# Two dense layers after attention: late part in units of 512 tokens, first product by seven half products, new priorities

## Chip, cores and metric

The kernel runs on one core of a Trainium2 chip. The metric is the device time of one execution in microseconds. The kernel before takes 1067.36 us, the median of three runs (1065.95 to 1068.06).

## The reference

Attention over 4 batches, 8 heads, 576 tokens and 64 elements a head, with a mask by blocks of 64 tokens, and then two dense layers on the 2304 tokens of all batches, 512 wide outside and 2048 wide inside. The weights come as 64-bit floats.

```python
scores = np.where(block_i >= block_j, scale * q @ k.T, -1e9)     # per batch and head, blocks of 64
attn = softmax(scores); x = (attn @ v), heads side by side       # (2304, 512)
# layer 1
h = x @ w_in                                                     # (2304, 512) @ (512, 2048)
g = np.maximum(h, 0.0) + alpha * np.minimum(h, 0.0)
x = g @ w_out                                                    # (2304, 2048) @ (2048, 512)
# layer 2, with weights of its own and no alpha
h = x @ w_in
g = h * (1.0 / (1.0 + np.exp(-1.702 * h)))
out = g @ w_out
```

## The kernel before

**Precision.** A matrix product is done as three: each operand is split into a high part and a low part (`hi_part`, L119, a ScalarE copy into the matmul's format; `lo_part`, L122, the difference, on VectorE or GpSimd), and high x high, high x low and low x high are added up in PSUM. A weight tile is loaded as 64-bit words (`load_w`, L132), made into 32-bit floats by one ScalarE and three VectorE instructions (`narrow`, L142) and split (`split_w`, L160).

**Stages.** The 2048 inner columns are 16 tiles of 128, counted by f. Under attention, layer 1 is done for f = 0 to 7 on blocks of 288 tokens (`gemm1`, L199, into tile `h`; `gate`, L211; `gate_split`, L222; `g2_half`, L237, into tile `x`); this partial sum of x goes to DRAM (`xa`). The late part follows: layer 1 for f = 8 to 15 and then layer 2 for all 16 f, both in six units of 384 tokens. A unit loads its input (`load_x`, L178), splits it whole (`split_x`, L184), and for each f runs 12 matmuls of the first product (four row blocks of 128, three splittings, 384 columns each, L207), the gate, the split of the gated tile, and the second product (`g2`, L636, matmuls at L653: four output tiles of 384 columns in layer 1, three of 512 columns in layer 2). `block_out` (L655) adds `xa` and stores to `x2s` in layer 1, or stores to `out` in layer 2.

**Buffers.** The late part has its own pools, which open when attention's close (`swap_pools`, L618). First products go to four PSUM banks in turn (`bank`, L195), second products gather in four more. Weight tiles of f = 0 to 7 lie in a pool of the whole kernel, those of f = 8 to 15 in a late one, and layer 2's tiles take over layer 1's places one by one.

**Order of the work.** Each step is entered with a planned place n and a kind (`at`, L115). The program is first written in the order of n; buffers of a ring are handed out in that order. Then `arrange` (L782) orders the instructions of every engine anew: it plays the program through with estimated costs (`cost`, L758) and, whenever an engine is free, takes from its ready instructions the one whose place, n + 0.1 x ORDER + SHIFT of its kind, is lowest. All DMAs are issued by SyncE (SP), in the order that this gives. While attention starts, "warm" matmuls (L579) on a constant tile fill TensorE.

Of the kernel before, what the change touches and what calls it, by code (L numbers as in the profile page):

```python
# [42 lines left out]
    "setup": 0, "swap": 0, "score": 1, "pv": 2, "prep t": 2.5, "warm": 2.6, "gemm1": 3, "gemm1 2": 3, "half": 3, "gemm2": 3.2, "soft": 3.5,  # L43
# [5 lines left out]
    "gate": -5.6, "gate 2": 3.5, "gemm1": 58, "gemm1 2": 12.5, "gemm2": 12.5, "half": 55.1, "half out": -40.2,  # L49
    "high": 14.8, "load alpha": 30.8, "load k": 48.3, "load q": -16.4, "load v": -13.4, "load w": 42,  # L50
    "load w 2": -8.5, "load x": 21.6, "narrow": 49, "narrow 2": 21.5, "norm": -15, "out": -55.1,
    "prep out": 29.6, "prep t": 14.3, "prep v": 33.9, "pv": 8.2, "pv out": -26.5, "rest": 11.7, "score": 53.6,
    "setup": -59.4, "soft": 5.6, "split g": -25.7, "split g 2": 33.6, "split w": 22.7, "split w 2": 22.6,
    "split x": 28.2, "split x 2": -47.3, "warm": 59.1,
# [5 lines left out]
def kernel(  # L60
# [21 lines left out]
    QB = 28  # L82
# [5 lines left out]
    NG = 6  # L88
    TA = 288
    TB = 384  # L90
    NB = NT // TB
# [15 lines left out]
    x2s = dram.tile([DM, NT], F32, name="x2s")  # L107

# [33 lines left out]
    def narrow(u):  # L142

        src = words[u]
        wi = src.bitcast(I32).rearrange("p (n t) -> p n t", t=2)
        wf = src.bitcast(F32).rearrange("p (n t) -> p n t", t=2)
        sq = raw.tile([128, 512], F32, tag="sq", name="sq")
        act.activation(out=sq, in_=wf[:, :, 1], func=ACTF.Copy, scale=2.0 ** -112)  # L150
        hi = sq.bitcast(I32)
        a = raw.tile([128, 512], I32, tag="wa", bufs=1, name="wa")
# [16 lines left out]
    def plan_w(z, u, n, lo, lag=2):  # L169
        at("load w" + z, n, lambda: load_w(u))  # L170
        at("narrow" + z, n + lag, lambda: narrow(u))
        at("split w" + z, n + lag + 1, lambda: split_w(u, lo))
# [3 lines left out]
    pend = {}  # L176

    def load_x(key, src, t0, n, pl, z):  # L178

        xl = pl.tile([128, KD, S if pl is blk else TB], F32R, tag=f"xl{z}", name="xl")[:, :, 0:n]  # L180
        sp.dma_start(out=xl.bitcast(F32), in_=src[:, t0:t0 + n].rearrange("(c p) t -> p c t", p=128))
        xb[key] = (xl.bitcast(F32), None, xl, n)

    def split_x(key, pl, z, lo, c=slice(0, KD)):  # L184
        r, xh, xl, n = xb[key]
        if xh is None:
            xh = pl.tile([128, KD, TB], F32R, tag=f"xh{z}", name="xh")[:, :, 0:n]
# [22 lines left out]

    def gate(key, layer, f):  # L211
        ps, n = pend[key, f]
        g = tmp_p.tile([128, TB], F32, tag="g", name="g")[:, 0:n]
# [8 lines left out]
    def gate_split(key, f, lo):  # L222
        g, n = pend.pop((key, f))

        w, z = (TA, f % NA) if key[0] == 0 else (TB, f % NG)
# [23 lines left out]
    def g2_half_out(key, d, t0, n):  # L249
        o = tmp_p.tile([128, TB], F32, tag="g", name="xo")[:, 0:n]  # L250
# [15 lines left out]
    def plan_x(i, n_split):  # L266
        def f(c):
# [4 lines left out]
            split_x((0, i), blk, 0, pool, slice(c, c + 1))  # L272
# [306 lines left out]
    def warm(cols):  # L579

        if "warm" not in st:
            st["warm"] = bank("warm")
        for _ in range(cols):
            pe.matmul(st["warm"], mk_l, mk_l.unsqueeze(1).to_broadcast([128, 3, 128]), start=True, stop=True)
# [30 lines left out]
    pb = ExitStack()  # L615
    late = {}

# [9 lines left out]
    NR = NF - NA  # L627
    for z in range(2 * NR):
        plan_w(" 2", (0, NA + z % NR, z // NR), t_end - QS + QA * z // NR, dve if z % 2 else pool)

    units = [(1, j) for j in range(NB)] + [(2, j) for j in range(NB)]
    seq = [(u, f) for u in units for f in (range(NA, NF) if u[0] == 1 else range(NF))]
    n2 = t_end + WT
    accs = {}

    def g2(u, f):  # L636
        layer, j = u
        gh, gl = gt.pop((u, f))
        oh, ol = W[layer - 1, f, 1]
        f0 = NA if layer == 1 else 0  # L640
        nd = KD if layer == 1 else TB // 128
        if f == f0:
            accs[u] = [late["o"].tile([128, DM], F32, tag=f"o{d}", name="acc") for d in range(nd)]
        for d in range(nd):
            sl = slice(128 * d, 128 * d + 128)
            if layer == 1:
                ps = accs[u][d][:, 0:TB]
                ops = ((oh[:, sl], gh), (oh[:, sl], gl), (ol[:, sl], gh))
            else:
                ps = accs[u][d]  # L650
                ops = ((gh[:, sl], oh), (gh[:, sl], ol), (gl[:, sl], oh))
            for z, (a, b_) in enumerate(ops):
                pe.matmul(ps, a, b_, start=f == f0 and z == 0, stop=f == NF - 1 and z == 2)  # L653

    def block_out(u):  # L655
        layer, j = u
        for d, ps in enumerate(accs.pop(u)):
            o = late["x"].tile([128, DM], F32, tag="o", bufs=2, name="o")
            if layer == 1:
                t = o[:, 0:TB]  # L660
                at_ = (slice(128 * d, 128 * d + 128), slice(TB * j, TB * (j + 1)))
                sp.dma_start(out=t, in_=xa[at_])
                dve.tensor_tensor(out=t, in0=ps[:, 0:TB], in1=t, op=ALU.add)  # L663
                sp.dma_start(out=x2s[at_], in_=t)
            else:
                act.activation(out=o, in_=ps, func=ACTF.Copy)  # L666
                sp.dma_start(out=out[TB * j + 128 * d:TB * j + 128 * d + 128, :], in_=o)

    LG = 2
    start = {}  # L670
    for z, (u, f) in enumerate(seq):
        n = n2 + z
        start.setdefault(u, n)
        plan_g1(" 2", n, u, u[0] - 1, f, pool)
        at("gemm2", n + LG, lambda u=u, f=f: g2(u, f))
        if f == NF - 1:
            at("out", n + LG + 1, lambda u=u: block_out(u))
    for y, u in enumerate(units):
        n = start[u]
        z = (y + 1) % 2  # L680
        at("load x", n - 6, lambda u=u, z=z: load_x(u, xs if u[0] == 1 else x2s, TB * u[1], TB, late["x"] if z else blk, z))
        at("split x 2", n - 3, lambda u=u, z=z: split_x(u, late["x"] if z else blk, z, dve))
    n3 = start[(2, 0)]
    for z in range(2 * NA):
        plan_w(" 2", (1, z // 2, z % 2), n3 - QB + QC * z // NA, dve if z % 2 else pool, 1)
    for z in range(2 * NR):
        plan_w(" 2", (1, NA + z // 2, z % 2), n3 - NR + z // 2 + 2 * (z % 2), dve if z % 2 else pool, 1)
# [70 lines left out]
def cost(eng, kind, ins, outs):  # L758
# [3 lines left out]
    if eng == "PE":  # L762
# [3 lines left out]
        each = 13.3 if mv.dtype == F32R else 2.7  # L766
        return cols / 2.4 + each, load / 1.2 + 13.3 if BYTES[w.dtype] == 4 else load / 4.8, cols * rows / 128, mode(w)
# [186 lines left out]
```

## Time and profile before

| | |
|---|---|
| median of three runs | 1067.36 us |
| span of the profiled execution | 1064.0 us, mean granted TensorE clock 0.988 |
| time of the profiled execution beside its span | not given apart; the runs' median lies 3.4 us above the span |
| instructions | 17161 |
| busy: TensorE matmul / weight load | 1014.2 / 931.0 us |
| busy: VectorE / ScalarE / GpSimd | 576.4 / 561.5 / 363.6 us |
| DMA | 120.28 MB, 47% of 16 engines' time |

One execution was profiled, and all rows come from it. Times are from the first instruction on. L207 is line 207 of the kernel. PE is TensorE's matmuls, PEld its weight loads, DVE VectorE, ACT ScalarE, POOL GpSimd, SP SyncE. Matmuls are pipelined, so the duration of one overlaps the next; the distance of their starts is what one costs. A tile's name stands without its number.

### The profile page before, as it was taken

How to read it: one execution, taken by the hardware profiler on the slowest of the kernel's cores; microseconds unless marked ns; L12 is line 12 of the kernel's file. 1: busy time of each engine (PE TensorE's matmuls, PEld its weight loads, DVE VectorE, ACT ScalarE, POOL GpSimd, SP SyncE). 2: the span in 40 equal slices, each digit the busy share in tenths (PEclk: the TensorE clock that was granted, in tenths of full speed). 3: DMA queues.
4: the chain of work that ended last, by engine and by line, in shares of the span. 5: the costliest groups of instructions: out<-in, count | busy, mean ns of one | idle time of the engine just before them, and what ended most of it. 6: DMA issues, size and time to landing. Idle time of an engine off the chain costs nothing.

```text
span 1064.0 us, 17161 instructions
## 1 busy us (share of the span) xinstructions
PE 1014.2 (95%) x6454; PEld 931.0 (87%) x6454; DVE 576.4 (54%) x1029; ACT 561.5 (53%) x1324; POOL 363.6 (34%) x334
## 2 busy tenths in 40 slices
PE   7777889989999999999999999999999999999998
PEld 4555788979899999999999999999999999999997
DVE  7899898678877756778872247822111121111110
ACT  6787888778888865554542335423232232322222
POOL 3354523223323435544442244422222222222221
PEclk8999999989999999999999999999999999999999
DMA  8899899899978764445551234401010010100000
GB/s 186 187 223 203 188 208 188 176 158 167 181 158 161 153 141 127 152 152 178 182 194 60 89 107 147 148 1 60 1 50 11 1 60 1 51 10 1 30 1 30
DMA packets 257283, 120.28 MB, mean 113 GB/s; under 512 B 213936, under 2 KB 250800, under 8 KB 257200
## 3 DMA queue, kind: packets, MB, share of 16 engines
q1 hardware_dynamic: 257200, 119.18, 47.0%
q8 instruction: 51, 0.84, 0.3%
q14 instruction: 32, 0.26, 0.1%
HBM read 68.82 MB, written 18.87 MB: 82 GB/s over the span
## 4 chain that ended last, share of the span: by engine, by line
PE 64%; DMA 1%; DVE 1%; ACT 1%; issue 0%; ACTq 0%; DVEq 0%
PE h L207 31%; PE acc L653 28%; PE x L245 1%; PE x L246 1%; PE x L247 1%; PE pv L519 1%; DMA xa<-xo 1%; PE sc L441 0%; DMA out_dram<-o 0%; DVE hl L494 0%; DVE g L216 0%; ACT hl L484 0%; ACT o L666 0%; DVE wl L123 0%; DVE wa L153 0%
## 5 line engine op out<-in xcount | busy, mean ns | idle before, releaser
L123 POOL TENSOR_TENSOR gs<-g,gs 128x384 fp32r<-128x384 f32 (+1 forms) x208 | 222.8, 1072 | 483.8 <-ACT gs L120 475.5
L207 PE MATMUL h<-xh,wh 128*128 128x384 f32 (+1 forms) x832 | 271.2, 326 | 6.1 <-ACT xh L120 3.4
L207 PE MATMUL h<-xh,wl 128*128 128x384 f32 (+1 forms) x832 | 269.5, 324 | 0.0
L219 DVE TENSOR_TENSOR g<-g,h 128x384 f32<-128x384 f32 x96 | 53.1, 553 | 301.8 <-ACT g L218 301.8
L653 PE MATMUL acc<-wh,gs 128*128 128x512 f32 x576 | 194.6, 392 | 0.0
L207 PE MATMUL h<-xl,wh 128*128 128x384 f32 x576 | 193.1, 335 | 0.0
L207 PEld LDWEIGHTS h<-xh,wh 128*128 128x128 f32 x832 | 156.2, 188 | 14.5 <-ACT xh L120 4.5
L218 ACT ACTIVATE g<-h 128x384 f32<-128x384 f32 x96 | 47.2, 492 | 213.7 <-PE h L207 210.0
L207 PEld LDWEIGHTS h<-xh,wl 128*128 128x128 f32 x832 | 156.3, 188 | 0.1
L120 ACT ACTIVATE gs<-g 128x384 fp32r<-128x384 f32 (+1 forms) x208 | 103.4, 497 | 83.8 <-DVE g L219 50.0
L653 PEld LDWEIGHTS acc<-wh,gs 128*128 128x128 f32 x576 | 108.1, 188 | 20.3 <-DVE o L663 0.2
L653 PE MATMUL acc<-wl,gs 128*128 128x512 f32 x288 | 113.7, 395 | 0.0
L207 PEld LDWEIGHTS h<-xl,wh 128*128 128x128 f32 x576 | 108.1, 188 | 4.1
L216 DVE SCALAR_TENSOR_TENSOR g<-g,nalph,h 128x288 f32<-128x288 f32 (+1 forms) x112 | 61.7, 552 | 71.0 <-ACT g L215 69.1
L653 PE MATMUL acc<-gs,wh 128*128 128x384 f32 x384 | 97.5, 334 | 0.0
L519 PE MATMUL pv<-pt,vp 128*128 128x256 f16 (+2 forms) x960 | 84.5, 242 | 8.9 <-DMA pt<-hl 7.6
L215 ACT ACTIVATE g<-h 128x288 f32<-128x288 f32 (+1 forms) x112 | 49.0, 440 | 83.2 <-PE h L207 75.5
L494 DVE SCALAR_TENSOR_TENSOR hl<-e,stat,hl 64x64 f16<-64x64 f32 (+4 forms) x160 | 89.5, 591 | 5.1 <-ACT hl L484 3.8
L123 POOL TENSOR_TENSOR wl<-sq,wh 128x512 fp32r<-128x512 f32 x40 | 58.6, 1464 | 97.1 <-ACT wh L120 92.4
L464 ACT ACTIVATE e<-sc,stat 64x64 f32<-64x64 f32 (+4 forms) x160 | 82.4, 517 | 5.6 <-DVE stat L456 5.1
L484 ACT ACTIVATE hl<-e,stat 64x64 f16<-64x64 f32 (+4 forms) x160 | 78.2, 551 | 9.8 <-DVE stat L474 4.6
L519 PEld LDWEIGHTS <-vp 128*128 128x128 bf16 x960 | 62.5, 99 | 20.0 <-DMA pt<-hl 9.5
(65 smaller groups left out, 1735.2 us busy)
## 6 DMA issues: line engine op xcount, KB each, us to landing
rw<-in_moe_w_in_dram SPq DMA_DIRECT2D x32, 512.0 KB, 3.9
rw<-in_moe_w_out_dram SPq DMA_DIRECT2D x32, 512.0 KB, 3.6
nat_q<-in_q_dram SPq DMA_DIRECT2D x24, 288.0 KB, 4.1
nat_k<-in_k_dram SPq DMA_DIRECT2D x16, 288.0 KB, 3.3
nat_v<-in_v_dram SPq DMA_DIRECT2D x16, 288.0 KB, 3.8
xa<-xo SPq DMA_DIRECT2D x32, 144.0 KB, 2.1
o<-xa SPq DMA_DIRECT2D x24, 192.0 KB, 2.4
xl<-xs SPq DMA_DIRECT2D x6, 768.0 KB, 4.4
```

The source lines that it names most:

```text
L120: act.activation(out=dst, in_=src, func=ACTF.Copy, scale=scale_)
L123: eng.tensor_tensor(out=dst, in0=src, in1=hi.bitcast(F32), op=ALU.subtract)
L207: pe.matmul(ps, st_[:, sl], mv[:, c], start=z == 0, stop=z == 3 * KD - 1)
L215: act.activation(out=g, in_=ps, func=ACTF.Relu, scale=-1.0)
L216: dve.scalar_tensor_tensor(out=g, in0=g, scalar=nalph[:, f:f + 1], in1=ps, op0=ALU.mult, op1=ALU.add)
L218: act.activation(out=g, in_=ps, func=ACTF.Sigmoid, scale=1.702)
L219: dve.tensor_tensor(out=g, in0=g, in1=ps, op=ALU.mult)
L464: act.activation(out=eo, in_=v[:, h] if len(heads) > 1 else v, func=ACTF.Exp, scale=-1.0, bias=stat[0:m, 0, a:a + 1], accum_out=stat[0:m, ...
L484: act.activation(out=o, in_=e, func=ACTF.Copy, scale=r)
L494: dve.scalar_tensor_tensor(out=hl_part(j, 1, m, nk, h), in0=es[h][0:m, off:off + nk], scalar=stat[0:m, 2, 2 * a + h:2 * a + h + 1], in1=hl ...
L519: pe.matmul(o, l, r, start=z == 0, stop=z == len(ops) - 1)
L653: pe.matmul(ps, a, b_, start=f == f0 and z == 0, stop=f == NF - 1 and z == 2)
```

## The change

Three parts, which come together.

*Units and first product.* The late units have 512 tokens (four of them and a last one of 256), and the f are taken in pairs. For a pair the weights form 2 x 2 blocks: rows of the input width in two halves, columns the two f; the unit's input forms 2 x 2 blocks of its row halves and of its two halves of 256 tokens. Strassen's scheme gives the four blocks of the result from seven products of combinations in place of eight. Four products (`first_half`) go to the two banks of a pair, a copy and two sums are taken from there (`snap`, ScalarE and GpSimd), three more products are added into the same banks (`second_half`), and VectorE adds the copies (`sums`). Each product is 2 row blocks x 3 splittings of 256 columns. The unit of 256 tokens needs four products. The second product now has 512 columns in layer 1 as well, and is planned two jobs (a job is a pair on a unit) behind the first.

*Combinations.* The seven combinations of a pair's weights are formed and split once on chip (`comb`) and stored to DRAM, 256 KB each. Layer 1's four pairs are fetched once and stay; layer 2's eight pairs are fetched anew for every unit into three slots that reuse places of older weights. The weights of layer 1's pairs are planned during attention (n = 75, 89, 103, 117; before at about 133). The input's seven combinations are formed for each unit (`comb_x`); its raw tile has one buffer, which the attention part uses too.

*Order.* Nearly all SHIFT values are new, those of attention and of the early blocks too, and `cost` counts a matmul of this format as 0.4515 ns a column and its weight load as 109 ns.

```diff
-    "gate": -5.6, "gate 2": 3.5, "gemm1": 58, "gemm1 2": 12.5, "gemm2": 12.5, "half": 55.1, "half out": -40.2,
...
+    "comb 2": 305.0, "comb 3": -66.8, "first": -168.3, "gate": -94.1, "gate 2": -2.7, "gemm1": 32.1,
...
-    NG = 6
+    NG = 4
     TA = 288
-    TB = 384
-    NB = NT // TB
+    TB = 512
+    TH = TB // 2
...
+    def comb(l, j, i):
+        a, b = (words[l, f, 0] for f in fpair(l, j))
+        a11, a12, a21, a22 = a[:, 0:256], a[:, 256:512], b[:, 0:256], b[:, 256:512]
+        two_ = {0: (a11, a22, ALU.add), 1: (a21, a22, ALU.add), 4: (a11, a12, ALU.add), 5: (a21, a11, ALU.subtract),
+                6: (a12, a22, ALU.subtract)}
...
+        t = slot(j, i) if kept else raw.tile([128, 2, 256], F32R, tag="wc", bufs=2, name="wc")
+        lo = pool if i % 2 else dve
...
+            (dve if i % 2 else pool).tensor_tensor(out=r, in0=x, in1=y, op=op)
...
+        hi_part(t[:, 0], r)
+        lo_part(lo, t[:, 1], r, t[:, 0])
...
+            sp.dma_start(out=wcs[l][j][i], in_=t.bitcast(F32).rearrange("p h c -> p (h c)"))
...
+    def load_wc(p):
...
+        for i in range(7):
+            if n == TB or i in (2, 3, 5, 6):
+                t = slot(j if l == 0 else (p - P2) % NSL, i)
+                sp.dma_start(out=t.bitcast(F32).rearrange("p h c -> p (h c)"), in_=wcs[l][j][i])
...
+    UO = (0, 1, 4, 2, 3), (0, 1, 2, 3, 4)
...
+    def load_x(u):
+        l, t0, n, key = u
+        xr = blk.tile([128, KD, TB], F32, tag="xl0", name="xr")[:, :, 0:n]
...
+    def comb_x(u, i):
...
+                x = late["x"].tile([128, 2, TH], F32, tag="xt", bufs=2, name="xt")
+                y, y2, op = two_[i]
+                pool.tensor_tensor(out=x, in0=y, in1=y2, op=op)
...
+        pl, tag = (blk, ("xlb", "xh0")[i]) if i < 2 else (late["x"], f"xc{i}")
+        t = pl.tile([128, 2, 2, TH], F32R, tag=tag, name="xc")
+        hi_part(t[:, 0], x)
+        lo_part(dve, t[:, 1], x, t[:, 0])
...
+    def prod(ps, p, i, y, first, last):
...
+        for c in range(2):
+            sl = slice(128 * c, 128 * c + 128)
+            for st_, mv in ((w[:, 0, sl], x[:, 0, c]), (w[:, 0, sl], x[:, 1, c]), (w[:, 1, sl], x[:, 0, c])):
+                pe.matmul(ps, st_, mv, start=first and z == 0, stop=last and z == 5, skip_group_check=True)
...
+    def first_half(p):
+        g, e = bank("ga"), bank("ep")
...
+            prod(g[:, 0:TH], p, 0, 0, True, False)
+            prod(g[:, TH:TB], p, 2, 2, False, True)
+            prod(e[:, 0:TH], p, 1, 1, True, False)
+            prod(e[:, TH:TB], p, 5, 5, False, True)
...
+    def snap(p):
...
+            act.activation(out=u, in_=g, func=ACTF.Copy)
+            act.activation(out=v, in_=e[:, 0:TH], func=ACTF.Copy)
+            pool.tensor_tensor(out=v, in0=u[:, TH:TB], in1=v, op=ALU.subtract)
+            pool.tensor_tensor(out=u[:, 0:TH], in0=u[:, 0:TH], in1=v, op=ALU.add)
...
+    def second_half(p):
...
+            prod(g[:, 0:TH], p, 6, 6, False, False)
+            prod(g[:, TH:TB], p, 4, 4, False, True)
+            prod(e[:, 0:TH], p, 3, 3, False, True)
...
+    def sums(p):
...
+            dve.tensor_tensor(out=u[:, TH:TB], in0=el, in1=v, op=ALU.add)
+            dve.tensor_tensor(out=u[:, TH:TB], in0=u[:, TH:TB], in1=gr, op=ALU.subtract)
+            dve.tensor_tensor(out=er, in0=er, in1=u[:, 0:TH], op=ALU.add)
+            dve.tensor_tensor(out=gl, in0=gl, in1=u[:, TH:TB], op=ALU.add)
...
+    seq_w = [(QB + QD * j, 0, j, None) for j in range(NPAIR[0])]
+    seq_w += [(t_end + 0.5 + y, 0, None, NA + y) for y in range(NR)]
+    n3 = start[2, 0]
+    seq_w += [(t_end + NR + 1 + (n3 - t_end - NR - 4) * j / NPAIR[1], 1, j, None) for j in range(NPAIR[1])]
+    seq_w += [(n3 - QC + 2 * f if f < NA // 2 else n3 + f - NA // 2, 1, None, f) for f in range(NF)]
...
-        each = 13.3 if mv.dtype == F32R else 2.7
-        return cols / 2.4 + each, load / 1.2 + 13.3 if BYTES[w.dtype] == 4 else load / 4.8, cols * rows / 128, mode(w)
+        time = cols * 0.4515 if mv.dtype == F32R else cols / 2.4 + 2.7
+        return time, load / 1.2 + 2.5 if BYTES[w.dtype] == 4 else load / 4.8, cols * rows / 128, mode(w)
```

## Rows read from the trace of the kernel before

**Rows 1.** Stretches: length, busy us (instructions) of each engine, TensorE clock, DMA share, GB/s.
```profile
0.00:105.00 105.00, 77.12 (x512) 52.20 (x513) 90.82 (x169) 76.66 (x194) 42.76 (x45) 0.92 0.92 198
105.00:404.00 299.00, 283.89 (x2397) 264.73 (x2396) 232.06 (x502) 243.90 (x673) 101.05 (x101) 0.99 0.86 170
...
454.00:664.00 210.00, 209.50 (x1209) 208.78 (x1209) 131.92 (x181) 92.81 (x171) 83.43 (x65) 1.00 0.43 139
664.00:1064.00 400.00, 394.91 (x1978) 357.02 (x1976) 82.06 (x127) 117.78 (x224) 105.83 (x98) 1.00 0.09 30
```
**Rows 2.** Chain of waits, 878 to 888 us: start, length, what.
```profile
878.99 2.10 PE h L207 x12
881.10 2.08 PE acc L653 x9
883.18 2.10 PE h L207 x12
```
**Rows 3.** Groups by line, TensorE: shapes, count, busy us, mean ns, idle before.
```profile
L653 PE MATMUL acc<-wh,gs 128*128 128x512 f32 x576 | 194.6, 392 | 0.0
L207 PE MATMUL h<-xh,wl 128*128 128x384 f32 x576 | 193.6, 336 | 0.0
L653 PE MATMUL acc<-gs,wh 128*128 128x384 f32 x384 | 97.5, 334 | 0.0
...
L207 PEld LDWEIGHTS h<-xl,wh 128*128 128x128 f32 x576 | 108.1, 188 | 4.1
```
**Rows 4.** Timeline of TensorE, 308.5 to 311 us: start, length, engine, line, tiles, shape.
```profile
308.65 0.60 PE L345 MATMUL tp<-ident,nat_q 128*128 128x128 f32 x4
...
309.69 0.29 PE L247 MATMUL x<-gs,wl 128*128 128x288 f32 x1
...
310.89 0.29 PE L247 MATMUL x<-gs,wl 128*128 128x288 f32 x1
```
**Rows 5.** Line 345 alone: duration ns min/median/max, first and last start us.
```profile
L345 PE MATMUL tp<-ident,nat_q x152: 270/273/473, 10.4 to 364.4; 128*128 128x128 f32 x152
```
**Rows 6.** Groups by line, the other engines, whole span.
```profile
L123 POOL TENSOR_TENSOR gs<-g,gs 128x288 fp32r<-128x288 f32 x64 | 60.7, 953 | 114.8 <-ACT gs L120 111.1 <-PE h L207 3.4
L123 POOL TENSOR_TENSOR wl<-sq,wh 128x512 fp32r<-128x512 f32 x40 | 58.6, 1464 | 97.1 <-ACT wh L120 92.4 <-PE acc L653 2.9 <-DMA nat_v<-in_v_dram 1.7
...
L155 DVE SCALAR_TENSOR_TENSOR wa<-sq,wa 128x512 int32<-128x512 int32 x64 | 61.2, 957 | 1.2
...
L153 DVE TENSOR_SCALAR wa<-sq 128x512 int32<-128x512 int32 x64 | 43.4, 678 | 11.5 <-ACT sq L150 10.4
L532 DVE SCALAR_TENSOR_TENSOR x<-pv,x 64x256 f32<-64x256 f32 x32 | 13.7, 427 | 22.0 <-ACT x L531 21.3
...
L666 ACT ACTIVATE o<-acc 128x512 f32<-128x512 f32 x18 | 10.7, 596 | 11.7 <-DMA out_dram<-o 7.8 <-PE acc L653 3.1
```
**Rows 7.** Tile xlb alone: duration ns min/median/max, first and last start us.
```profile
L207 PE MATMUL h<-xlb,wh x256: 288/294/429, 43.8 to 446.2; 128*128 128x288 f32 x128
L123 POOL TENSOR_TENSOR xlb<-x,xh x32: 790/816/1662, 42.7 to 426.8; 128x288 fp32r<-128x288 f32 x32
```
**Rows 8.** Line 247 alone, the last of a block's second product.
```profile
L247 PE MATMUL x<-gs,wl x256: 288/295/402, 128.7 to 462.6; 128*128 128x288 f32 x128
```
**Rows 9.** Stretches, line 153 on VectorE alone, one instruction for each weight tile narrowed.
```profile
0.00:400.00 400.00, 11.63 (x18) 0.97 0.88 179
400.00:470.00 70.00, 8.81 (x14) 1.00 0.47 146
```
**Rows 10.** DMA issues: count, KB each, median us from issue to landing.
```profile
xl<-xs SPq DMA_DIRECT2D x6, 768.0 KB, 4.4
...
out_dram<-o SPq DMA_DIRECT2D x18, 256.0 KB, 2.0
```
**Rows 11.** Timeline of TensorE at the end, 1052 to 1064 us.
```profile
1052.42 0.33 PE L207 MATMUL h<-xh,wl 128*128 128x384 f32 x1
...
1058.53 0.39 PE L653 MATMUL acc<-wh,gs 128*128 128x512 f32 x1
```

More of the change, by code (lines that the diff above doesn't have):

```diff
@@ L42 @@
 ORDER = {
-    "setup": 0, "swap": 0, "score": 1, "pv": 2, "prep t": 2.5, "warm": 2.6, "gemm1": 3, "gemm1 2": 3, "half": 3, "gemm2": 3.2, "soft": 3.5,
+    "comb 2": 6.5, "comb 3": 6.5, "load w 3": 9, "narrow 3": 7, "split w 3": 5.9, "load wc": 8.8, "first": 3, "second": 3, "snap": 2.7, "sums": 3.9, "setup": 0, "swap": 0, "score": 1, "pv": 2, "prep t": 2.5, "warm": 2.6, "gemm1": 3, "gemm1 2": 3, "half": 3, "gemm2": 3.2, "soft": 3.5,
     "out": 3.8, "gate": 4, "gate 2": 4, "pv out": 4.5, "prep out": 4.7, "norm": 5, "high": 5.1, "half out": 5, "split w": 5.9,
@@ L626, with fpair @@
     at("swap", t_end, swap_pools)
[L627 to L633, printed above, removed]
-    accs = {}
[L636 to L643, printed above, removed]
+    def fpair(l, j):
+        f = 2 * j + (NA if l == 0 else 0)
+        return f, f + 1
@@ new lines, in load_wc @@
+    def load_wc(p):
+        l, (_, t0, n, _), j = jobs[p]
+        if l == 0 and j in wc0:
+            wc[p] = wc0[j]
+            return
+        ts = []
+        for i in range(7):
+            if n == TB or i in (2, 3, 5, 6):
+                t = slot(j if l == 0 else (p - P2) % NSL, i)
+                sp.dma_start(out=t.bitcast(F32).rearrange("p h c -> p (h c)"), in_=wcs[l][j][i])
+            else:
+                t = None
+            ts.append(t)
+        wc[p] = ts
+        if l == 0:
+            wc0[j] = ts
@@ L644, in g2 @@
+    accs = {}
+    def g2(u, f, first, last):
+        l, _, n, key = u
+        gh, gl = gt.pop((key, f))
+        oh, ol = W[l, f, 1]
+        nd = KD if l == 0 else n // 128
+        if first:
+            accs[key] = [late["o"].tile([128, DM], F32, tag=f"o{d}", name="acc") for d in range(nd)]
         for d in range(nd):
             sl = slice(128 * d, 128 * d + 128)
-            if layer == 1:
-                ps = accs[u][d][:, 0:TB]
+            if l == 0:
+                ps = accs[key][d][:, 0:n]
@@ L678 @@
[L678 to L687, printed above, removed]
+    place = []
@@ new lines @@
+    n = n2
+    for p, (l, u, j) in enumerate(jobs):
+        start.setdefault(u[3], n)
+        place.append(n)
+        n += 2 if u[2] == TB else 1
+    place += [n, n + 1, n + 2, n + 3]
+    for p, (l, u, j) in enumerate(jobs):
+        n, key = place[p], u[3]
+        at("load wc", place[max(p - 2, 0)] - 4 * (p < 2), lambda p=p: load_wc(p))
+        at("first", n, lambda p=p: first_half(p))
+        at("snap", n + 0.3, lambda p=p: snap(p))
+        at("second", n + 0.9, lambda p=p: second_half(p))
+        at("sums", n + 1.3, lambda p=p: sums(p))
+        for y, f in enumerate(fpair(l, j)):
+            z = 2 * (p % 2) + y
+            at("gate 2", n + 1.4, lambda key=key, l=l, f=f: gate(key, l, f))
+            at("split g 2", n + 1.4, lambda key=key, f=f, z=z: gate_split(key, f, pool, z))
+            at("gemm2", place[p + 2] + 0.1 + 0.1 * y, lambda u=u, f=f, a=j == 0 and y == 0, b=j == NPAIR[l] - 1 and y == 1: g2(u, f, a, b))
+        if j == NPAIR[l] - 1:
+            at("out", place[p + 2] + 0.4, lambda u=u: block_out(u))
```

167 lines of the change are left out of this document (128 added, 39 removed).

## The prediction

> **What bounds the kernel now.** I read the table of stretches first [rows 1]. From 454 us to the end TensorE is busy 209.5 of 210 us and 394.9 of 400 us at a granted clock of 1.00 (the 2.4 GHz level), while VectorE, ScalarE and GpSimd are busy for 21 to 63% of these stretches. From 105 to 404 us TensorE is at 95%, ScalarE at 82%, VectorE at 78% and the DMA engines at 86%: there everything is tight, and the clock is 0.99. Only the first 105 us hold much idle TensorE time (28 us). The chain of waits says the same of the late part: 12 first products, 9 second products, 12, 9, with nothing between [rows 2]. So the late part is as long as its matmuls. The groups by line [rows 3] give their number: first product (L207) 3 x 576 = 1728 of 384 columns, second product (L653) 384 and, of its low weights, half as many again, 576 of 384 columns in layer 1, and 576 + 288 = 864 of 512 columns in layer 2.
>
> **Spacing of matmuls.** "Mean ns of one" (336, 392) overlaps its neighbours and is no price. The distance of starts is: 12 of 384 columns lie between 878.99 and 881.10 us, which is 175.8 ns each (period 4.19 us less 2.08, by 12), and 9 of 512 columns in 2.08 us, 231.1 ns each [rows 2]. Nine intervals of 288 columns in a loaded stretch span 309.69 to 310.89 us: 133.3 ns each [rows 4]. Per column that is 0.458, 0.451 and 0.463 ns: time goes with columns, with no visible constant.
>
> **The change, part by part.**
>
> *First product.* A pair of 128-wide slices of the hidden layer on 512 tokens needs 7 half products x 2 row blocks x 3 splittings = 42 matmuls of 256 columns, where the direct form has 24 of 512. The last unit of a layer has 256 tokens and takes 4 products, 24 matmuls. Layer 1 has 4 pairs, layer 2 has 8: 12 x (4 x 42 + 24) = 2304 matmuls of 256 columns (589,824 columns against 663,552). No matmul of 256 columns in this format is in the trace. From below its spacing is bounded by four transposes of 128 columns, which end 0.60 us after their first start and last 0.273 us each: (0.60 - 0.273)/3 = 109 ns [rows 4, 5]. From above by 133.3 ns, the spacing at 288. I take 117.2, which is 256 x 0.458, the price of the row at 384, the nearest that nothing disturbs (by the row at 288 it would be 118.5). Before: 1728 x 175.8 = 303.8 us. After: 2304 x 117.2 = 270.0 us (251 to 307). Gain 33.8 us (53 to a loss of 3). This is on the path, as nothing else fills the late part.
>
> The Trainium skill, page "TensorE: Matmul & The Clock Gate", section "Back-to-back issue gap", puts the warm gap at N/2.4 + 2.5 ns; this case's rows of 384 and 512 columns lie 8 and 7% above that. By the page the sum would be 1728 x 162.5 = 280.8 before and 2304 x 109.2 = 251.6 after, a gain of 29 us.
>
> *Second product.* Layer 1: 384 of 512 and 96 of 256 columns, 88.7 + 11.3 = 100.0 us, where 576 x 175.8 = 101.3 us stood. Layer 2 keeps 864 of 512. A gain of 1.3 us (0 to 2), which I count as nothing.
>
> *Evictions.* A full job (a pair on a unit) now has two copies on ScalarE and two GpSimd operations between its halves, and four VectorE operations before its gates. What hides this is the second product of the job two back, 24 x 231 ns = 5.5 us, which TensorE does meanwhile; a copy from PSUM of 512 columns takes 0.60 us [rows 6], so the wait between the halves is about 1.3 us with its signals. Four banks hold two jobs; a job takes 42 x 117.2 + 24 x 231.1 ns = 10.5 us. Its banks must be free again after one whole job of the other pair of banks; the chain after its second half (4 x 0.43 for the sums by the 256-column row, gates of about 0.6 on ScalarE and 0.85 on VectorE, twice a row of 256) is some 4 us. Covered, 0 us. Without the cover it would be 1.3 us in each of 48 full jobs, 62 us.
>
> *Loads on the other engines in layer 1.* Its late part will last 16 x 10.5 + 4 x 5.6 = 190 us. GpSimd: 32 low parts of 512 columns at 1.46 us, 32 differences of 256 at 0.85 (scaled from 288 at 0.953), 20 input sums at 1.46, 48 operations of layer 2's combinations at 0.85, some 6 weight splits and the small unit's low parts: 160 us, or 84% [rows 6]. VectorE: 54 us of sums and gates (3.4 a full job), some 26 weight tiles to narrow at 0.68 + 2 x 0.96 = 2.6 us [rows 6], the input's low parts 20, the combinations 19, the outputs 13: near 182 us if all of it fell in this stretch, though pairs 2 to 7 may come during layer 2, where a job needs only 3.4 of 10.5 us. It fits, with little room. I charge the nine changes of unit for this: the new input needs four of its seven combinations (about 4.5 us by these rows) within the 7.6 us of second product and second half that stand between its first use and the old one. In layer 1 the three that start on a busy GpSimd I put at 1.5 us each: 5 us in all (0 to 20).
>
> *Into the late part.* The input buffer of a unit is now the one that the last attention batch leaves, and two combinations lie where the last early block has its split input. Those splits are made up to 427 us, and its last first product starts at 446 [rows 7]; after it 16 us of second halves are left, to 462.6 us [rows 8]. Load (4.4 us, [rows 10]) and combinations fit beneath. 0 us (0 to 6).
>
> *Under attention.* The 8 weight tiles of layer 1's pairs and their 28 combinations have to be ready when the late part starts. So far 18 of the 64 tiles are narrowed before 400 us and 14 from 400 to 470 [rows 9]; the eight now have to come earlier: 8 x 2.6 us on VectorE, 28 combinations with some 9, 11 and 20 us on VectorE, ScalarE and GpSimd, and 14.7 MB to DRAM and back. From 105 to 404 us VectorE has 67 us free, ScalarE 55, GpSimd 198 [rows 1]. New priorities order all of it again. From below a gain: the TensorE time lost in the first 404 us is 43 us. From above a loss: 30 us if all VectorE work of it were added to attention. As it fits the gaps by rows I take 2 us of loss.
>
> *Reload in layer 2.* Each job fetches its seven combinations of 256 KB: 256 fetches, 67.1 MB, with inputs, outputs and weights 84.9 MB in 1536 x 117.2 + 864 x 231.1 ns = 379.7 us, or 224 GB/s. From 454 to 664 us the queue moved 139 GB/s at a share of 0.43, so 323 GB/s at full share; from 105 to 404 us, with short packets, 170 at 0.86, so 198 [rows 1]. The new packets are of 2 KB, like the outputs that land in 2.0 us [rows 10] and the stretch from 454 on, so I take 323: 263 of 380 us, hidden, with three slots of buffer. 0 us (0 to 49).
>
> The Trainium skill, page "DMA: Bandwidth & Descriptors", section "Bandwidth", asks for 1 MiB in a transfer and gives 138 GB/s at 64 KB and 341 at 1 MB; 256 KB would be about 240 by an estimate between them. That would still be hidden, 354 of 380 us, but with far less room than the rows give.
>
> *The end.* The last first product starts at 1052.42 us and the last second one at 1058.53 [rows 11]; a small last unit leaves 12 instead of 9 second products behind it and one eviction less. 0 us.
>
> Sum on the profiled execution: 1064.0 - 33.8 + 5 + 2 = 1037.2 us. The median of the runs, 1067.36, is 3.4 us above that span (the page shows no other time of this execution), so **1041 us**.
>
> **Rivals.**
>
> 1. *Weight load sets the pace at 256 columns.* A load of 128 columns lasts 188 ns in the rows [rows 3], longer than the new spacing, and two of them must overlap. For it: no 256-column row. Against: at 288 columns loads of 188 ns already go at 133 ns, at 128 columns matmuls at 109. At 125 ns, halfway to the upper bound, 2304 x 7.8 = 18 us are lost: 1059.
>
> 2. *Reload bounds layer 2 (slower).* If the fetches run at the 198 GB/s of the loaded stretch, layer 2 takes 84.9 MB/198 = 429 instead of 380 us: 1041 + 49 = 1090. It decides below 224 GB/s. Against: short packets made that rate, and these are long.
>
> 3. *Layer 1's combinations come late (slower).* Two buffers carry them; a step (0.85 + 0.4 + 0.85 us, then 2.0 us to land) takes about 2.3 us, a pair with its two narrowings 21. If they begin only at 404 us, as 14 of 16 tiles did before, the pairs end at 488 us, and the eight tiles of the second product behind them in the same buffers at 510, where gemm2 wants the first at 464: up to 45 us, 1086. It costs the whole gain from a delay of 26 us on. Against: the gaps of VectorE and ScalarE named above.
>
> 4. *The new order shortens the early part.* Of the 43 us lost there a quarter, 11 to 12 us, comes back: 1029. For it: 28 us lie in the first 105, where warm-up matmuls run beside. Against: VectorE and DMA at 86 and 92% there.
>
> **How the numbers follow.** Forecast 0.63 (1030 to 1053), rival 1 0.08, rival 2 0.05, rival 3 0.12, rival 4 0.12. The range reaches from rival 4's side to just under the time before: 1026 to 1066; beyond it lie rival 2, most of rival 3 and a little of rival 4. A measurement of this kernel tells about 0.2% (2 us) from no change. Faster: 0.63 + 0.12 + 0.07 + a quarter of rival 3 = 0.85; the same 0.03; slower 0.12.
>
> **What would show it.** Late first products 117 ns apart, 42 and 24 to a job of 10.5 us; TensorE near 100% from about 460 us; layer 2's DMA share near 0.7 with no TensorE wait for a fetch; late part some 33 us shorter and its start within 10 us of 454. Wrong: a spacing above 122 ns, waits for combination tiles, or TensorE gaps at the unit changes of more than 2 us each.

## Result and profile after

The changed kernel takes 1079.13 us, the median of four runs (1077.71 to 1083.54), against 1066.98 us for the kernel before on the same chip: a ratio of 1.0114, interval 1.0089 to 1.0139. It was forecast at 1041 and is slower by 12 us. The profiled execution has a span of 1077.3 us.

The table of stretches of the changed kernel, to be laid beside [rows 1] (same columns):

```profile
0.00:105.00 105.00, 75.76 (x478) 51.77 (x479) 86.29 (x163) 73.32 (x187) 41.28 (x45) 0.87 0.86 194
105.00:404.00 299.00, 274.97 (x2277) 252.52 (x2275) 253.21 (x539) 251.30 (x695) 115.35 (x119) 0.97 0.94 198
475.00:600.00 125.00, 119.02 (x804) 109.45 (x803) 99.97 (x150) 63.80 (x139) 87.69 (x86) 1.00 0.57 187
600.00:700.00 100.00, 95.60 (x614) 86.05 (x614) 73.97 (x121) 50.27 (x99) 69.05 (x66) 1.00 0.79 268
700.00:800.00 100.00, 94.45 (x580) 82.78 (x579) 75.69 (x113) 49.74 (x91) 58.86 (x48) 1.00 0.77 261
800.00:1070.00 270.00, 269.29 (x1656) 241.50 (x1656) 84.33 (x162) 99.70 (x193) 111.77 (x108) 1.00 0.52 164
```

Three things are to be seen. From 105 to 404 us TensorE started 2277 matmuls where it had started 2397: attention and the early blocks run late. From 475 to 800 us it is short of full in every row, where nothing was missing before. From 800 us on it is full, and the DMA engines are at 0.52.

The early part ends with the second product of the last early block, which [rows 8] put at 462.6 us. The same line alone, in the changed kernel:

```profile
L253 PE MATMUL x<-gs,wl x256: 288/296/382, 139.0 to 483.2; 128*128 128x288 f32 x128
```

So the early part ends 20.6 us later. (This line, one row in each kernel, is the measure of the early part in all that follows. Some late products already run ahead of it: about 6 us of them in the kernel before and in the changed one.) The last first product over the old input buffer moved alike, from 446.2 [rows 7] to 467.5:

```profile
L208 PE MATMUL h<-xlb,wh x256: 290/296/442, 45.6 to 467.5; 128*128 128x288 f32 x128
```

The late part, from the first late product to the last second product, went from 604.4 us (454.2 to 1058.5) to 598.9 (474.5 to 1073.4), not to some 575. Its groups by line are as counted beforehand, 1368 + 936 = 2304 half products and 864 second products of layer 2 (576 in the third line, 288 more with the low weights):

```profile
L740 PE MATMUL ga<-xc,ws 128*128 128x256 f32 x1368 | 188.6, 284 | 8.7 <-ACT u L764 4.1 <-DVE g L222 2.2 <-DVE g L225 1.9
L740 PE MATMUL ep<-xc,ws 128*128 128x256 f32 x936 | 132.2, 284 | 4.0 <-ACT xc L126 1.6 <-DVE g L225 1.3 <-ACT v L765 0.8
L815 PE MATMUL acc<-wh,gs 128*128 128x512 f32 x576 | 182.8, 392 | 2.2 <-DVE o L825 1.9 <-ACT o L828 0.3
```

Their distances are read from the chain of waits in the dense stretch (start, length, what), as in [rows 2]:

```profile
884.97 1.44 PE ga L740 x12
886.41 0.72 PE ep L740 x6
887.13 4.11 PE acc L815 x18
891.24 1.43 PE ga L740 x12
```

Twelve of 256 columns take 1.44 us, 120 ns each; 18 of 512 columns take 4.11 us, 228.3 ns each. From these the late part without a gap would be 2304 x 0.120 + 1248 x 0.2283 + 96 x 0.120 = 276.5 + 284.9 + 11.5 = 572.9 us. So 26 us of the 598.9 are stalls (some 2 us of these are early products that still run between the first late ones). The rows of 475 to 800 us show 15.9 us as idle (325 less 119.02, 95.60 and 94.45); most of the rest hides in "busy", since one matmul is shown with 284 ns for a distance of 120.

How one such stall comes about, from the chain of waits around 685 us:

```profile
682.11 0.32 SPq L688
682.52 0.48 SPq L688
683.09 4.56 DMA wc<-wc
687.78 0.75 POOL wc L647
688.58 0.30 issue
688.88 0.96 ACT sq L156 x2
689.99 0.59 ACT g L224
690.58 0.28 ACT v L765
690.91 0.98 PE ep L740 x6
```

SyncE issues fetches of reloaded combinations (L688, the last two are shown), and only then the store of a freshly formed one (wc<-wc, L655). That store takes 4.56 us to land; until then its buffer isn't free, GpSimd can't write the next combination (L647), ScalarE, whose order is fixed, stands behind GpSimd, and behind that stand a gate (g) and the copy out of PSUM (v) that TensorE's second half needs. TensorE waits 0.81 us here. Over 475 to 800 us ScalarE and VectorE wait along this way, and ScalarE for raw weight tiles (rw) too (engine, line, waited for: us in total, times, longest):

```profile
ACT wc L126 <- POOL wc L647: 23.4, 12, 7.7
ACT sq L156 <- DMA rw<-in_moe_w_out_dram: 21.8, 12, 4.5
...
DVE wc L129 <- ACT wc L126: 19.3, 15, 2.7
```

The first and the last line belong to the forming; its last store starts at 690.1 us, so nothing is formed from 700 us on. The middle line is another matter: 19.5 of its 21.8 us lie between 700 and 800 us. There ScalarE waits for raw tiles of layer 2's second product, which SyncE loads among the fetches.

The DMA issues of 600 to 700 us (count, KB each, us to landing) show fetches and stores beside each other, and the output rows that were to be their price, 2.0 us in [rows 10], far off:

```profile
ws<-wc SPq DMA_DIRECT2D x47, 256.0 KB, 4.2
wc<-wc SPq DMA_DIRECT2D x21, 256.0 KB, 3.4
```

From 475 to 600 us, with seven fetches only, the stores landed in 2.2 us (median), and TensorE had stalls all the same.

Early, the wait that is new lies between 200 and 250 us. That stretch of before and of after (columns as in [rows 1]):

```profile
200.00:250.00 50.00, 44.59 (x368) 40.36 (x367) 38.78 (x87) 40.19 (x116) 15.30 (x17) 0.93 0.88 158
```
```profile
200.00:250.00 50.00, 38.65 (x302) 33.51 (x302) 41.56 (x90) 39.62 (x116) 14.86 (x16) 0.86 0.97 208
```

66 matmuls fewer, and the granted clock falls with the idle time, from a mean of 0.93 to 0.86 (between the levels of 1.2 and 2.4 GHz). TensorE's own waits there say for what: the scores of the next attention step stand behind ScalarE's exponentials of an earlier one, first before, then after:

```profile
PE sc L441 <- ACT e L464: 0.4, 1, 0.4
```
```profile
PE sc L447 <- ACT e L470: 9.2, 4, 4.4
```

### The profile page after: what moved, and what is told of

Same layout as the page of the kernel before. It is cut to its first block, busy times and chain, and to the rows that moved or that the text cites. A ratio compares the mean times of both kernels' runs of the same rounds, so it can differ in the third digit from the quotient of the medians.

```text
span 1077.3 us, 19739 instructions
## 1 busy us (share of the span) xinstructions
PE 1001.1 (93%) x6934; PEld 892.5 (83%) x6934; DVE 722.1 (67%) x1313; ACT 627.2 (58%) x1492; POOL 522.9 (49%) x506
## 4 chain that ended last, share of the span: by engine, by line
PE 49%; DMA 11%; ACT 7%; DVE 7%; issue 3%; POOL 2%; SPq 0%; ACTq 0%; POOLq 0%; DVEq 0%
PE acc L815 20%; PE ga L740 12%; PE ep L740 8%; DMA wc<-wc 4%; DMA rw<-in_moe_w_out_dram 3%; DMA pt<-hl 2%; PE pv L525 2%; PE sc L447 2%; ACT hl L490 2%; PE h L208 2%; ACT e L470 1%; POOL gs L129 1%; PE x L251 1%; PE x L252 1%; DVE g L222 1%
## 5 line engine op out<-in xcount | busy, mean ns | idle before, releaser
L129 POOL TENSOR_TENSOR gs<-g,gs 128x512 fp32r<-128x512 f32 (+2 forms) x184 | 208.0, 1135 | 207.2 <-ACT gs L126 171.4
L740 PE MATMUL ga<-xc,ws 128*128 128x256 f32 x1368 | 188.6, 284 | 8.7 <-ACT u L764 4.1
L740 PEld LDWEIGHTS ga<-xc,ws 128*128 128x128 f32 x1368 | 177.5, 191 | 18.4 <-ACT u L764 4.8
L126 ACT ACTIVATE gs<-g 128x512 fp32r<-128x512 f32 (+2 forms) x184 | 98.1, 536 | 83.7 <-PE acc L815 65.8
L740 PE MATMUL ep<-xc,ws 128*128 128x256 f32 x936 | 132.2, 284 | 4.0 <-ACT xc L126 1.6
L740 PEld LDWEIGHTS ep<-xc,ws 128*128 128x128 f32 x936 | 122.8, 191 | 10.4 <-DVE g L225 2.8
L815 PE MATMUL acc<-gs,wh 128*128 128x512 f32 (+1 forms) x320 | 94.5, 371 | 1.8 <-DVE o L825 1.8
L208 PE MATMUL h<-xh,wh 128*128 128x288 f32 x256 | 78.0, 305 | 5.2 <-ACT xh L126 2.6
L251 PE MATMUL x<-gs,wh 128*128 128x288 f32 x256 | 76.7, 302 | 0.9 <-ACT gs L126 0.4
L252 PE MATMUL x<-gs,wh 128*128 128x288 f32 x256 | 77.1, 302 | 0.3 <-POOL gs L129 0.3
L208 PE MATMUL h<-xh,wl 128*128 128x288 f32 x256 | 77.0, 301 | 0.0
```

The costliest lines, as they stand in the source:

```text
L126: act.activation(out=dst, in_=src, func=ACTF.Copy, scale=scale_)
L129: eng.tensor_tensor(out=dst, in0=src, in1=hi.bitcast(F32), op=ALU.subtract)
L208: pe.matmul(ps, st_[:, sl], mv[:, c], start=z == 0, stop=z == 3 * KD - 1)
L251: pe.matmul(ps, oh[:, sl], gh, start=f == 0, stop=False)
L252: pe.matmul(ps, oh[:, sl], gl, start=False, stop=False)
L740: pe.matmul(ps, st_, mv, start=first and z == 0, stop=last and z == 5, skip_group_check=True)
```

## Experiments

All kernels are built by the same planner, which writes out each engine's order. In the first four and the last three it plans anew after the edit. In the five called "order as in the changed kernel" or "order kept" the order is planned for the whole program first and then kept, instruction by instruction, while some of it is left out.

Where the stages ended, from the line of the early second product alone in each kernel and from the first and last late product (us):

| kernel | ratio of times | early part ends | late part |
|---|---|---|---|
| before | 1 | 462.6 | 604.4 |
| after | 1.0114 | 483.2 | 598.9 |
| after, old priorities | 1.0314 | 494.9 | 612.6 |
| before, new priorities | 1.0222 | 489.5 | 604.3 |
| layer 1 direct | 1.0326 | 488.4 (20 us of late products ahead) | 627.4 |
| four buffers | 1.0378 | 485.4 | 620.9 |
| three pairs not prepared in layer 1 | 1.0098 | 477.3 | 602.2 |
| layer 2's combinations not formed | 1.0003 | 482.4 | 587.0 |
| no reload | 1.0040 | 487.3 | 589.6 |
| no copies and sums | 1.0125 | 482.6 | 600.4 |
| neither forming nor reload | 0.9915 | 482.9 | 579.5 |
| before, nudged | 1.0167 | 481.7 | 608.4 |
| after, nudged (two draws) | 1.0251, 1.0210 | 482.5, 483.3 | 611.5, 606.4 |

**The old priorities in the changed kernel.**

```diff
 SHIFT = {   # 25 kinds of the early part
-    "gate": -94.1, "gemm1": 32.1, "half": 28.7, ...
+    "gate": -5.6, "gemm1": 58, "half": 55.1, ...
```

> The changed kernel with the old priorities for the 25 kinds of step that attention and the early blocks are made of. Theory A (the longer early part comes from the work brought under attention: eight weight tiles, 28 combinations and their transfers): the last early second product stays near 483 us (before 462, after 483), time 1079 +- 4 us. Rival B (it comes from the new order of the early steps): it goes back to about 463 us, time about 1059 us.

Measured: 1100.16 us (1097.06 to 1103.99), ratio 1.0314, interval 1.0274 to 1.0353; the early part ends at 494.9. Neither theory: the old priorities don't bring the old order back, as the planner places the added work among the same steps. Why this order is later still was not followed.

**The new priorities in the kernel before**, the same lines the other way round, with no work added.

> The kernel before with the new priorities for the same 25 kinds, nothing else. Theory A: the last early second product stays within 4 us of 462, time 1067 +- 4 us. Rival B: it moves to about 480 us, time about 1085 us.

Measured: 1089.63 us, ratio 1.0222, interval 1.0191 to 1.0253. The late part is as before (604.3 us); the early part alone is 26.9 us longer. An order planned from other priorities costs more here than the whole early loss of the change.

```profile
L247 PE MATMUL x<-gs,wl x256: 290/295/380, 146.6 to 489.5; 128*128 128x288 f32 x128
```

**Layer 1's late part direct**, in units of 512 tokens; the half products in layer 2 alone.

```diff
+        if l == 0:
+            for f, ps in zip(fpair(l, j), (g[:, 0:n], e[:, 0:n])):
+                h, lo = W[l, f, 0]
+                for c in range(KD):
...
-    seq_w = [(QB + QD * j, 0, j, None) for j in range(NPAIR[0])]
+    for y in range(NR):
+        plan_w(" 2", (0, NA + y, 0), t_end - QS + 0.8 * y, dve if y % 2 else pool)
```

> The changed kernel with layer 1's late part in the direct form (512-token units, 12 matmuls of 512 columns a tile, weights loaded and split where the kernel before does it); layer 2 keeps its half products. Theory A: with nothing added under attention the early part ends near 463 us. Rival B: near 480 us. Theory C (late stalls of 26 us come from forming layer 2's combinations through two buffers, which blocks the in-order engines): TensorE still loses 10 us or more during layer 1. Rival D (they come from the copies and sums of each job): less than 5 us there. Time by A and C about 1060 us, by A and D about 1049, by B 1069 or more.

Measured: 1100.77 us, ratio 1.0326, interval 1.0303 to 1.0349. With no combination formed or stored under attention the early part ends at 488.4, later than in the changed kernel. But here its last steps stand behind 88 late products, where the changed kernel has 54 of half the length. Two of four lines, from 460 us to the end of the early part (columns as in [rows 3]):

```profile
L766 PE MATMUL ga<-xd,wd 128*128 128x512 f32 x48 | 11.4, 390 | 0.0
L836 PE MATMUL acc<-gs,wh 128*128 128x512 f32 x20 | 6.2, 389 | 0.0
```

At 228.3 ns these 88 are 20 us. By this estimate the early part alone takes 468 us, against 477 in the changed kernel (54 x 120 ns = 6.5 us taken off) and 456 in the one before (36 x 175.8 ns = 6.3 us taken off): without the added work it is 8 us shorter than in the changed kernel and still 12 us longer than before. The order is another one, so this doesn't settle how the 20.6 us divide. Theories C and D stay open as well: TensorE is busy for 120.63 of 125 us from 475 to 600 us and 96.20 of 100 to 700, and loses most, 18.2 us, between 700 and 800.

**Two more buffers for layer 2's combinations.**

```diff
-        t = slot(j, i) if kept else raw.tile([128, 2, 256], F32R, tag="wc", bufs=2, name="wc")
+        t = slot(j, i) if kept else raw.tile([128, 2, 256], F32R, tag="wc", bufs=2, name="wc") if l == 0 else \
+            (raw.tile([128, 2, 256], F32R, tag="wc", bufs=2, name="wc") if i % 2 else
+             late["x"].tile([128, 2, 256], F32R, tag="wd", bufs=2, name="wc"))
```

> The changed kernel with four buffers in place of two for the combinations of layer 2's weights (two of them from the late pool). Theory C: the stalls of TensorE between 475 and 800 us fall from about 26 us to about 10, time about 1063 us. Rival D: they stay, time 1079 +- 4 us.

Measured: 1107.34 us, ratio 1.0378, interval 1.0339 to 1.0418, the slowest of all. The plan moved everywhere (the early part ends at 485.4, the late one is 22 us longer), so the run tells nothing of the buffers. After these four I kept the order fixed.

**Order as in the changed kernel; three of layer 1's four pairs not prepared.** Left out: six weight tiles, 21 combinations and what of these is stored; layer 1 uses the first pair's in their place.

```diff
     def comb(l, j, i):
+        if planned and (l, fpair(l, j)[0], 0) in left_out:
+            return
```

> The changed kernel with every engine's order kept, but three of layer 1's four pairs are not prepared (6 of 8 weight tiles loaded and narrowed, 21 of 28 combinations and their stores left out; the fetches read the first pair's instead, so the numbers are wrong). Theory A (the added work holds attention up): the last early second product comes 12 to 20 us earlier, at 463 to 471 us. Rival B (the new order of the early steps is itself slower, whatever stands in the gaps): at 478 to 484 us, and the time stays within 5 us of 1079.

Measured: 1077.47 us, ratio 1.0098, interval 1.0036 to 1.0160; the early part ends at 477.3, 5.9 us earlier. Kernels with the same order and the same early work end it at 482.4, 482.6, 482.9, 483.2 and 487.3, so the 5.9 are little more than what one execution differs from another. That is just outside both theories' bands, and much nearer to B's. Up to 404 us more had been won, 63 of the 120 matmuls by which the changed kernel's row was short:

```profile
105.00:404.00 299.00, 280.13 (x2340) 258.92 (x2339) 241.10 (x515) 249.04 (x682) 103.11 (x104) 0.98 0.85 172
```

The wait of 200 to 250 us stayed, although the DMA share of that stretch fell from 0.97 to the 0.88 of the kernel before:

```profile
PE sc L453 <- ACT e L476: 8.6, 4, 4.1
```

From 213 to 240 us no engine takes a step of the weights in this run, and the two long waits lie there. So neither traffic nor work on weights in this stretch makes the scores wait; ScalarE goes through attention's and the early blocks' steps in its fixed order, with the exponentials behind others. The first pair's combinations, formed just ahead, from 160 to 212 us, were not taken out. The new priorities alone don't bring the wait either: in the kernel before with new priorities it is 1.0 us, and that kernel loses its time elsewhere. The late part did not gain: layer 1's combinations are there in time.

**Order kept; layer 2's pairs not prepared.** Left out: 16 weight tiles, 56 combinations and their stores; the same number of fetches reads layer 1's. The edit is the one above, for the other layer.

> The changed kernel with every engine's order kept, but layer 2's pairs are not prepared (16 weight tiles, 56 combinations and their stores left out; the same number of fetches reads layer 1's combinations, so the numbers are wrong). Theory C (forming them blocks the in-order engines): the late part shrinks from 599 to 580 us or less, time about 1060. Rival D (each job's copies and sums): it stays within 5 us of 599.

Measured: 1067.35 us, ratio 1.0003, interval 0.9979 to 1.0027; late part 587.0, 12 us shorter, which lies between the two theories. From 475 to 600 us TensorE is nearly full now; from 700 to 800 us it isn't, and ScalarE's wait for raw weight tiles has stayed:

```profile
475.00:600.00 125.00, 124.07 (x853) 115.50 (x853) 55.94 (x102) 49.46 (x100) 63.79 (x61) 1.00 0.25 80
700.00:800.00 100.00, 97.10 (x605) 86.42 (x606) 70.47 (x109) 48.94 (x90) 59.34 (x49) 1.00 0.75 250
```
```profile
ACT sq L162 <- DMA rw<-in_moe_w_out_dram: 18.5, 9, 3.7
```

**Order kept; layer 2 fetches for its first three jobs alone** and uses those combinations on.

```diff
     def load_wc(p):
+        if planned and p >= P2 + NSL:
+            wc[p] = held[p % NSL]
+            return
```

> The changed kernel with every engine's order kept; layer 2 fetches its combinations for the first three jobs only and reuses these three sets (numbers wrong, 60 MB less moved). If the transfers of the reload are what TensorE and the other queues wait for: the late part shrinks by 10 us or more, most of it between 700 and 800 us. Theories C and D: by less than 4 us.

Measured: 1072.98 us, ratio 1.0040, interval 1.0008 to 1.0073; late part 589.6, 9.3 us shorter, a little under the 10 expected. The row of 475 to 600 us is as it was, and most of the gain lies between 700 and 800 us:

```profile
475.00:600.00 125.00, 118.95 (x800) 109.36 (x799) 98.69 (x147) 63.37 (x138) 88.11 (x85) 1.00 0.57 188
600.00:700.00 100.00, 97.51 (x633) 89.42 (x633) 76.67 (x123) 52.03 (x103) 70.77 (x68) 0.98 0.60 203
700.00:800.00 100.00, 99.04 (x620) 88.93 (x619) 78.26 (x119) 51.54 (x94) 62.22 (x51) 1.00 0.33 106
```

The waits over 475 to 800 us show what went: not ScalarE's wait for the forming (23.4 us in the changed kernel), but the one for raw weight tiles (21.8).

```profile
ACT wc L127 <- POOL wc L648: 22.1, 10, 8.4
...
ACT sq L157 <- DMA rw<-in_moe_w_out_dram: 4.3, 5, 1.6
```

**Order kept; no copies out of PSUM between the halves and no sums.** The gates read the banks as they are.

```diff
     def snap(p):
+        if planned:
+            return
```

> The changed kernel with every engine's order kept, without the copies and differences between the halves and without the sums after them (numbers wrong). Rival D: the late part shrinks by 15 us or more. Theory C: by less than 8 us.

Measured: 1081.48 us, ratio 1.0125, interval 1.0091 to 1.0158; late part 600.4. Beside the other stalls, which stayed, all of the recombination costs nothing that can be measured, though the copies are the last to release TensorE in many a wait: they pass on what held ScalarE.

**Order kept; neither forming nor reload**, the two edits together.

> Every engine's order as in the changed kernel; left out: the forming of layer 2's combinations (16 tiles, 56 combinations, their stores) and every fetch of them after the first three jobs. Theory F (the forming and the fetches stall TensorE at different moments, so their 12 and 9.3 us add): the late part, first late product to last second product, goes from 599 to 576-581 us and the time to 1056-1062. Theory G (they are one stall that either of them is enough to cause or to cure): 585-590 us, time 1064-1070. If 576-581 comes, what is left over the products' own 572 us is the start of layer 1's late units.

Measured: 1058.57 us, ratio 0.9915, interval 0.9886 to 0.9944; late part 579.5. The two add (12 + 9.3 expected, 19.4 measured), and 6.6 us are left over the 572.9 of the products, some 2 of them early products. In these 6.6 us the copies and sums are included. TensorE after 475 us:

```profile
475.00:600.00 125.00, 124.07 (x853) 115.50 (x852) 56.22 (x101) 49.21 (x99) 62.83 (x60) 1.00 0.25 81
600.00:700.00 100.00, 99.85 (x635) 90.65 (x634) 59.68 (x99) 45.93 (x82) 55.03 (x49) 1.00 0.48 158
700.00:800.00 100.00, 98.92 (x622) 88.92 (x621) 68.90 (x105) 49.79 (x92) 61.76 (x51) 1.00 0.23 74
```

**The kernel before, its priorities nudged:** 28 kinds moved at random by up to two places, no work added.

```diff
-    "gate": -5.6, "gemm1": 58, "gemm2": 12.5, "half": 55.1, "load q": -16.4, ...
+    "gate": -7.1, "gemm1": 59.4, "gemm2": 13.6, "half": 54.1, "load q": -18.0, ...
```

> The kernel before with each of 28 kinds' priorities moved at random by up to two places; no work added, nothing else changed. Theory A (the early part's 20.6 us are mostly the price of a different written-out order, since the old one was a sharp choice): the last early second product starts 6-25 us later than 462.6, time 1073-1092. Theory B (orders near the old one are all about as good, and the added work is what costs): within 4 us of 462.6, time 1063-1071.

Measured: 1085.50 us, ratio 1.0167, interval 1.0138 to 1.0197. The early part ends at 481.7, 19.1 us later than 462.6, with nothing added (one draw was run):

```profile
L276 PE MATMUL x<-gs,wl x256: 288/295/445, 130.0 to 481.7; 128*128 128x288 f32 x128
```

**The changed kernel, nudged likewise, two draws.**

> The changed kernel with the same 28 random moves. Theory A: the time moves by 6-25 us, up or down, with no work added or taken away. Theory B: within 4 us of 1077.

> The changed kernel with another draw of 28 moves of up to two places. Theory A: the time moves by 6-25 us, up or down, and differs from that of the first draw by as much. Theory B: within 4 us of 1077.

Measured: 1094.45 us (ratio 1.0251, interval 1.0221 to 1.0281) and 1090.04 (1.0210, 1.0180 to 1.0239), 15 and 11 us slower than the changed kernel. The sizes are theory A's, though the two draws differ by 4 us and not by 6 or more. The place isn't: the early part ends at 482.5 and 483.3, where it did, and it is the late part that got 13 and 8 us longer, mostly from 700 to 800 us. There TensorE's weight loads for the second product now wait for the weights' high parts (first draw, 690 to 800 us; same columns as the waits above):

```profile
PEld acc L852 <- ACT wh L163: 5.2, 3, 2.7
```

Three of the moved kinds, "gemm2", "load x" and "out", belong to the late part; which of the moves did it was not tried.

## Why the prediction was wrong

The sum forecast a span of 1037.2 us; 1077.3 was measured. Two of its steps failed, about equally, and they make up the 40 us between:

*Under attention* was priced at 2 us because the added work fits the gaps of VectorE and ScalarE in [rows 1]; the early part ends 20.6 us later, 18.6 more than that. The added work was not the main thing to price. The kernel before ends this part at 462.6, and no other order of it that was run comes near: 489.5 and 481.7 without any added work, 482.5 to 494.9 in five orders with it (the changed kernel, its two nudged forms, the old priorities, the four buffers); layer 1 direct, without the work, comes nearest, 12 us behind when its late products are taken off. Work taken out of the new order gave at most 6 us. The sentence "New priorities order all of it again" stood in the prediction, but the loss for it was bounded by the added VectorE work alone, as if one order were as good as another. The table of stretches that I read first could have warned: with TensorE at 95% and three others at 78 to 86%, much is tight at once.

What is shown is that another order alone costs 19 and 27 us in the kernel before. That the changed kernel's own 20.6 is order for the most part is concluded from this, from the wait of scores for exponentials that stays when three pairs are taken out, and from the 6 us. The first pair was not taken out. Nor was it tried what the changed buffers do by themselves: narrowing now shares two buffers with the combinations, where it had one of its own.

*Loads on the other engines in layer 1* and *Reload in layer 2* were charged 5 and 0 us, and both argued by sums: GpSimd 84% of its stretch, 263 of 380 us of transfers. (The VectorE list adds up to 174 us where the prediction says 182; nothing hangs on it.) TensorE's gaps came from somewhere that neither step looked at. Forming layer 2's combinations, from about 475 to 690 us, makes ScalarE wait for GpSimd, and its fixed order hands the delay on to the gates and copies: 12.0 us less without it, and the row of 475 to 600 us full. Fetching them again, from 600 us on, delays the raw weight tiles of the second product in the same queue, and ScalarE waits for these: 9.3 us less without the fetches, most of it after the forming has ended. The runs show that each costs TensorE this much; that it goes by these waits is read from which of them vanish with which piece (23.4 to none, 21.8 to 4.3 us). How much of the forming's part is the landing of stores in its two buffers isn't shown, as the run with four buffers moved the order. Together 26 us of stalls stand in place of the 5; 19.4 go when both are left out. The 6.6 that remain were not divided further. The step about layer 2's steady state was right: from 800 us on TensorE is at 269.29 of 270 us with the DMA engines at 0.52.

*First product* had its size a little wrong: 120 ns for 117.2, so 2304 x 2.8 ns = 6.5 us. "No visible constant" was the mistake. The rows of 288 and 256 columns together, 133.3 [rows 4] and 120 ns, give 0.416 ns a column and a constant of 13 ns; with it 384 columns come to 173 (175.8 read in [rows 2]) and 512 to 226 (228.3 now). The prediction's price per column came from one row, at 384, and spread that row's constant over its columns, so that 256 columns came out too cheap. The Trainium skill, page "TensorE: Matmul & The Clock Gate", section "Back-to-back issue gap", gives N/2.4 + 2.5 ns for an isolated matmul, by estimate 109.2 here; its slope agrees with these rows, its constant is about 11 ns short of them.

*Second product* was counted as nothing and gave 4.6 us: 301.0 us before by the prediction's prices, 284.9 + 11.5 now, as 512 columns come at 228.3 ns against 231.1 [rows 2] and layer 1 has them too. The end is 1.6 us shorter (3.9 against 5.5 us after the last product starts), the first late product 0.3 further ahead of the last early one.

Sum: 18.6 + (26.0 - 5) + 6.5 - 4.6 - 1.6 - 0.3 = 39.6, of 40.1 us.

*Evictions* at nothing was right as far as the runs go: with every copy and sum left out the late part is no shorter, and with them in it 6.6 us are all that is left. *Into the late part* held too: once forming and reload are away, 475 to 600 us lacks 0.9 us. Rival 1 is ruled out (120 ns, with loads of 192 ns hidden under it). Rival 3 pointed at the combinations, but of the wrong layer: layer 1's combinations came in time, and layer 2's were the ones that cost. Rival 4 had the sign the other way round.

No version that does the whole computation beat the kernel before. With the preparation and the reload of layer 2 left out the changed kernel is at 0.9915 of before even with its slow early part; but that leaves out 16 weight tiles which the kernel before does prepare, so it only bounds what the half products could bring.

## What to carry to other kernels

When a change makes a planner write the order of a dense stretch anew, price the new order itself, as a term with its own bounds: nudging the old kernel's priorities, with nothing added, is one run and gives a first size of that term (19 us here, from one draw). Work that "fits the gaps" by sums over a stretch still has to be followed through the engines' fixed orders and the shared queue: here combinations that ScalarE had to wait for, and raw tiles loaded among fetches, held up gates and copies that had nothing to do with them. To find out what an added piece costs, keep every engine's order and leave the piece out; edits that let the order move again measured mostly the move. And look at what a marker stands behind: the end of a part counts whatever the planner has put ahead of it.

## What the runs showed of the hardware that was not expected

Matmuls in this format have a fixed part of about 13 ns each beside 0.416 ns a column at a granted clock of 1.00: 120 ns at 256 columns, 133.3 at 288, 228.3 at 512. Weight loads of 192 ns stay hidden at a distance of 120 ns.

Transfers of 256 KB in rows of 2 KB, which landed in 2.0 us in the quiet late part of before [rows 10], took 4.2 us (fetches) and 3.4 us (stores) with the DMA engines at 0.79, single ones up to 7.8 and 7.1 us. The rate is not what suffers: 268 GB/s at 0.79 is 339 at full share, above the 323 that the prediction used. The Trainium skill, page "DMA: Bandwidth & Descriptors", section "Bandwidth", gives the two figures from which the prediction's estimate of some 240 GB/s for this size came; the estimate lies below these rows, and the rows decide: 339 at full share by the stretch of 600 to 700 us, 315 by that of 800 to 1070 (164 at 0.52).
